# Pooled attention with a routed feed-forward layer: queries loaded as whole rows and half of them moved between partition groups, values loaded by one transfer

## The chip, the core and the metric

The kernel runs on one core of a Trainium2 chip. The metric is the device time of one execution in microseconds (us). The core has TensorE (PE in the profile; its weight loads are PEld), VectorE (DVE), ScalarE (ACT), GpSimd (POOL) and the queue of SyncE (SP), which issues nearly all transfers here. Each engine works through its own instructions in order; semaphores tie the engines together.

## What is computed

Eight batches of eight heads. The queries of neighbouring positions are averaged in twos (1152 rows become 576), attention is computed without a mask, and the result of all heads side by side (576 rows of 512) goes through a routed layer: a score for each row, and the 128 rows with the highest score get a gated two-layer feed-forward update.

```python
q_pool = q.reshape(B, H, S // 2, 2, D).mean(axis=3)        # B=8, H=8, S=1152, D=64
scores = q_pool @ k.T / sqrt(D)
x = softmax(scores) @ v                                    # -> (B, 576, 512)
s = x @ w_gate
top = argpartition(-s[b], 128)[:128]
out[b] = x[b];  out[b, top] += sigmoid(s[b, top]) * (relu(x[b, top] @ w1) @ w2)
```

## The kernel before

**Pairs and halves.** Two heads (j = 0, 1) of a batch make a pair; there are 32 pairs. The 128 partitions hold head j's 64 dimensions at rows 64j to 64j+63. A pair is worked in two halves, one for each 288 of its 576 pooled queries: half number h = 2n + s belongs to pair n, and s = 0 or 1 picks the columns of the transposed queries `qT`. I call halves with s = 0 even and those with s = 1 odd.

**One half, in the order of `run` (L1562).** The order on every engine is that in which this loop writes the instructions; nothing reorders them. In each half:
- `scores` (L853): PE multiplies the transposed keys `kT` with `qT` (columns of this half) in nine chunks of 128 keys, ACT exponentiates each chunk out of PSUM into `p` (L876). PSUM holds four such chunks.
- `side_by_side` (L938, even halves) or `spread` (L953, odd halves): four small ACT copies between groups of 32 partitions.
- `units("mid")`: pieces of the routing of an earlier batch, among them PE's feed-forward products.
- `gated` (L1035, DVE), then `folded` (L901): POOL adds two thirds of `p` (L908), DVE transposes and sums (L913, twice) and joins the sums (L923). These give the softmax denominators.
- `units("sums")`: more routing, then `multiplied` (L976, POOL).
- `added` (L944, DVE) and `prepare_pair` (L761) for the next pair, in even halves only.
- `weighted` (L878) of the half before: PE multiplies `p` with the values, ACT copies the result out of PSUM (L895), POOL adds its two parts (L897); `drained` (L966): DVE transposes it.
- `normalized` or `divided`, and `units("end")`: rank comparisons (L1145 to L1164) and searches (L1229) of the routing, on DVE.

So PE alternates between the scores of half h and the weighted sum of half h - 1, and `qT` and `kT` of pair n + 1 are made in pair n's even half, a whole half before PE first reads them.

**Loads.** `load_pair` (L735) is called in the odd half, for the pair after the next: four transfers for keys and four for queries, one for each group of 32 partitions (head j, dimensions 0 to 31 or 32 to 63). Each moves, for each of 32 partitions, 36 pieces of 32 numbers (128 bytes). `load_values` (L748) follows, four transfers of 32 partitions whose rows are whole (2304 bytes for each head), for the next pair. All are issued by SP. The first pair is loaded and prepared by other code (L776 to L851).

**Preparation.** `prepare_pair` adds neighbouring queries on POOL (L767: 128x576), transposes the keys in blocks of 32x32 on DVE (L770: 128x1152) into columns ordered (c, g, i), and the queries likewise (L774: 128x576). A block transposition stays within its group of 32 partitions, and since the load has put each group's own 32 dimensions there, the result lies where `scores` reads it. `kb`, `kT` and `qT` have two buffers each; `qb` and `qp` have one.

**Routing.** For each batch b the routing starts at half 8b + 10 and goes on in pieces for some twenty halves. Batches 0 to 5 are updated in twos, with seven block products on PE (L1437) in each layer, at halves 28 and 31, 44 and 47, 60 and the end. The transposition of the picked rows (L1284) stands in `units("sums")` of an odd half.

Of the kernel before, what the change touches and what calls it, by code (L numbers as in the profile page):

```python
# [10 lines left out]
P = 128  # L11
BLK = 32

G = 3
F32 = mybir.dt.float32
# [12 lines left out]
def _any_scores(  # L28
# [451 lines left out]
    in_pair = [(j, t) for j in range(2) for t in range(NF)] + [(0, NF)]  # L480
    upcoming = load_pair(*pairs[0])
    run(prepare_pair(upcoming))
    preparing = iter(())
    routing = iter(())
# [23 lines left out]
    for n, (b, hp) in enumerate(pairs):  # L508
        pair = upcoming
        run(preparing)  # L510
        if hp == 0:
            x = xpool.tile([P, NT, Dm], F32, name="x")
        for i, (j, t) in enumerate(in_pair):
            now = {"pair": pair, "j": j, "t": t, "x": x}
            advance(now)
            if two is not None and two["t"] == NF and two["pair"]["hp"] == NPAIR - 1:
                run(routing)
                routing = routed(two["pair"]["b"], two["x"])
            one, two = now, one
            if i == 0 and n + 1 < len(pairs):  # L520
                upcoming = load_pair(*pairs[n + 1])
                preparing = prepare_pair(upcoming)
            if n == 0 and i == 0:
                load_weights()
            if i >= 3:
                next(preparing, None)
            next(routing, None)
# [7 lines left out]
class _Plain:  # L535
# [199 lines left out]
    def load_pair(self, b, hp):  # L735

        nc = self.nc
        kb = self.load.tile([P, self.KB, BLK], F32, name="kb")
        qb = self.load.tile([P, self.QB, 2, BLK], F32, name="qb", bufs=1)
        for j, ds, rows in self.quarters():  # L740
            of = self.k[b, 2 * hp + j, :, ds]
            nc.sync.dma_start(kb[rows, :, :], of.rearrange("(i n) d -> i n d", i=BLK))
        for j, ds, rows in self.quarters():
            of = self.q[b, 2 * hp + j, :, ds].rearrange("(i m) d -> i m d", i=BLK)
            nc.sync.dma_start(qb[rows, :, :, :].rearrange("i n r d -> i (n r) d"), of)
        return {"k": kb, "q": qb, "b": b, "hp": hp}

    def load_values(self, pair):  # L748


        nc, hp = self.nc, pair["hp"]
        v_sb = pair["v"] = self.load.tile([P, 2, self.NC, self.D], F32, name="v_sb", bufs=2)
        of = self.v[pair["b"], 2 * hp : 2 * hp + 2]
        of = of.rearrange("j (i g c) d -> g i j c d", i=BLK, c=self.NC)
        for g in range(P // BLK):
            nc.sync.dma_start(
                v_sb[g * BLK : (g + 1) * BLK, :, :, :].rearrange("i j c d -> i j (c d)"),
                of[g].rearrange("i j c d -> i j (c d)"),
            )

    def prepare_pair(self, pair):  # L761

        nc = self.nc
        qp = self.load.tile([P, self.QB, BLK], F32, name="qp", bufs=1)
        kT = pair["kT"] = self.load.tile([P, self.S], F32, name="kT")
        qT = pair["qT"] = self.load.tile([P, self.Sp], F32, name="qT")
        nc.gpsimd.tensor_tensor(  # L767
            out=qp[:, :, :], in0=pair["q"][:, :, 0, :], in1=pair["q"][:, :, 1, :], op=ALU.add
        )
        nc.vector.transpose(  # L770
            kT.rearrange("p (c g i) -> p c g i", c=self.NC, i=BLK),
            pair["k"].rearrange("p (g c) d -> p c g d", c=self.NC),
        )
        nc.vector.transpose(qT[:, :], qp.rearrange("p n d -> p (n d)"))  # L774

    def load_first(self, b, hp):  # L776

# [784 lines left out]
    def run(self):  # L1562
        nc = self.nc
        pairs = [(b, hp) for b in range(self.B) for hp in range(self.NPAIR)]
        n_halves = 2 * len(pairs)
        halves = []
        self.routing, self.waiting = [], set()
        upcoming = self.load_first(*pairs[0])
        self.first_constants()
        self.prepare_first(upcoming)  # L1570
        self.constants()
        loaded = self.load_pair(*pairs[1]) if len(pairs) > 1 else None
        self.load_gate()
        weights = self.weight_loads()
        sums = self.weight_sums() if self.paired else iter(())
        for h in range(n_halves):
            n, s = divmod(h, 2)
            if s == 0:
                pair = upcoming
                if pair["hp"] == 0:  # L1580
                    part = self.ffn.tile([P, self.NPAIR, self.QB], F32, name="part")
                pair["part"] = part
            else:
                loaded = None
                if n + 2 < len(pairs):
                    loaded = self.load_pair(*pairs[n + 2])
                if n + 1 < len(pairs):
                    self.load_values(upcoming)
                if n > 1:
                    self.stored(halves[h - 4]["pair"])  # L1590
            if h > 1:
                next(weights, None)

            if 5 < h < 14 or 18 < h < 23:
                for _ in range(2 - s):
                    next(sums, None)
            half = {"pair": pair, "s": s}
            halves.append(half)
            self.scores(half)
            if h > 1:  # L1600

                of = halves[h - 2 - s]["pair"]
                if s == 0:
                    of["groups"] = self.side_by_side(of["sum"].rearrange("p j n -> p (j n)"))
                else:
                    self.spread(of)
            self.units("mid")
            if h > 2:
                self.gated(halves[h - 3])
            self.folded(half)  # L1610
            if h > 2:
                self.scored(halves[h - 3])
            self.units("sums")
            if h > 1:
                self.multiplied(halves[h - 2])
            if h > 1 and s == 0:
                last = halves[h - 1]["pair"]
                last["total"] = self.added(last["groups"])
            if s == 0 and loaded:
                upcoming = loaded  # L1620
                self.prepare_pair(upcoming)
            if h > 0:
                self.weighted(halves[h - 1])
                self.drained(halves[h - 1])
            if h > 2 and s == 1:
                self.normalized(halves[h - 2]["pair"])
            if h > 3 and s == 0:

                self.divided(halves[h - 3]["pair"])
            self.units("end")  # L1630
        for _ in weights:
            pass
        for _ in sums:
            pass

        def pieces(unit, n=None):
            for i, _ in enumerate(unit):
                if i + 1 == n:
                    break


        left = [unit for _, unit, _ in self.routing]
        old = left.pop() if left else iter(())
        older = left.pop() if left else iter(())
        assert not left
        self.gated(halves[-3])
        pieces(old, 1)
        self.weighted(halves[-1])
        self.drained(halves[-1])
        self.multiplied(halves[-2])  # L1650
        self.multiplied(halves[-1])
        self.scored(halves[-3])
        self.gated(halves[-2])
        pieces(older, 1)
        self.normalized(halves[-1]["pair"])
        self.gated(halves[-1])
        self.scored(halves[-1])
        _, new, _ = self.routing.pop()

        pieces(new, 1)  # L1660
        pieces(old, 1)
        for half in (halves[-3], halves[-1]):
            self.divided(half["pair"])
            self.stored(half["pair"])
        pieces(older, 2)
        pieces(new, 1)
        pieces(old, 1)
        pieces(older, 1)
        pieces(new, 3)
        pieces(older, 4)  # L1670
        pieces(old, self.NFC // 2)
        pieces(new, 1)
        low = self.counted()
        pieces(old, self.NFC // 2 + 1)
        pieces(older)
        pieces(new, 2)
        pieces(old)
        count = self.outside(low)
        pieces(new, 10)
        found = nc.values_load(count[0:1, 0:1])  # L1680
        E = mybir.EngineType
        self.tc.mark_branch_hint_location("again", found, [E.PE, E.DVE, E.Pool, E.Activation, E.SP])
        pieces(new)
        return found
# [61 lines left out]
```

## Time and profile before

| what | value |
|---|---|
| median of 3 runs | 689.82 us (689.19 to 692.28) |
| the profiled execution | 689.66 us |
| its span in the profile | 687.9 us |
| granted TensorE clock, mean | 0.998 |
| busy PE, PEld | 678.0 us (99%), 564.4 us (82%) |
| busy DVE, ACT, POOL | 536.4 us (78%), 457.7 us (67%), 512.9 us (75%) |
| DMA | 101.22 MB in 397,059 packets, 377,232 of them under 512 bytes |
| share of the 16 DMA engines' time, SP's queue | 67.1% |
| start of one half's scores to the next half's, undisturbed | 8.73 us |

The profile is one execution. A row of its groups gives line, engine and operation, what it writes and reads, partitions x elements, the count, the busy time, the mean duration in ns, and the idle time of the engine just before it with the instruction that ended that idle time. A row of its timeline gives start, duration, engine, line and operation, with idle time and releaser in brackets. An engine's next instruction often starts some 0.07 us before the listed end of the last one, so in a chain the distance of starts is what counts.

### The profile page before, as it was taken

The page shows a single profiled execution, that of the slowest core. Times are in us where ns is not written, and L with a number is a line of the kernel's source. Part 1 is how long each engine was busy: PE and PEld are TensorE (multiplying, and loading weights), DVE is VectorE, ACT ScalarE, POOL GpSimd, SP SyncE. Part 2 cuts the span into 40 slices and gives each one's busy share as a digit, 9 for nine tenths or more (in the row PEclk, how much of TensorE's full clock was granted, in tenths as well). Part 3 has the DMA queues.
Part 4 walks back from the last instruction along what each step waited for, and adds up shares of the span by engine and source line. Part 5 has one row for each costly group of instructions (what it writes and reads, how often), then busy time and mean ns, then how long its engine had stood idle before and what let it go on. Part 6 is the DMA issues. An engine that isn't in the chain of part 4 may idle for free.

```text
span 687.9 us, 23660 instructions
## 1 busy us (share of the span) xinstructions
PE 678.0 (99%) x9972; PEld 564.4 (82%) x9972; DVE 536.4 (78%) x842; ACT 457.7 (67%) x998; POOL 512.9 (75%) x503
## 2 busy tenths in 40 slices
PE   9999999999999999999999999999999999999996
PEld 6668899989997998786888899777788899867776
DVE  3867888998999796786698977695879989688930
ACT  5677777777777783847777677583877777575220
POOL 4788888798887775867996978483999888569241
PEclk9999999999999999999999999999999999999999
DMA  9888878688779767953878787783777777644311
GB/s 173 158 176 182 209 143 202 130 155 165 138 167 171 159 136 140 229 101 80 227 129 176 135 166 148 139 197 64 158 190 171 140 152 163 118 116 118 81 47 36
DMA packets 397059, 101.22 MB, mean 147 GB/s; under 512 B 377232, under 2 KB 381200, under 8 KB 395664
## 3 DMA queue, kind: packets, MB, share of 16 engines
q1 hardware_dynamic: 395408, 95.13, 67.1%
q0 software_dynamic: 1296, 4.20, 1.9%
q8 instruction: 80, 1.31, 0.8%
q10 hardware_dynamic: 240, 0.30, 0.2%
q14 instruction: 35, 0.29, 0.1%
HBM read 81.97 MB, written 17.62 MB: 145 GB/s over the span
## 4 chain that ended last, share of the span: by engine, by line
PE 83%; DVE 4%; DMA 4%; issue 4%; POOL 3%; ACT 1%; SPq 0%; POOLq 0%; DVEq 0%; ACTq 0%
PE ps L887 36%; PE ps L869 36%; PE ps L1437 8%; DVE fold L913 2%; DMA out_dram<-xe,index 1%; PE ps L1312 1%; POOL acc L908 1%; ACT p L876 1%; DMA v_sb<-in_v_dram 1%; DMA lines<-row_rank 1%; PE ps L616 1%; DMA row_rank<-both 0%; POOL prod L976 0%; POOL s L1403 0%; DVE pick L1164 0%
## 5 line engine op out<-in xcount | busy, mean ns | idle before, releaser
L876 ACT ACTIVATE p<-ps 128x576 f32<-128x576 f32 x576 | 320.4, 699 | 2.4 <-PE ps L869 2.4
L887 PE MATMUL ps<-p,v_sb 64*64 64x288 f32 x4608 | 296.7, 403 | 2.0 <-DMA v_sb<-in_v_dram 2.0
L869 PE MATMUL ps<-qT,kT 64*64 64x288 f32 x4608 | 296.4, 403 | 0.7 <-DVE token L637 0.5
L908 POOL TENSOR_TENSOR acc<-p 128x576 f32<-128x576 f32 x192 | 272.0, 1444 | 26.7 <-ACT p L876 26.1
L887 PEld LDWEIGHTS ps<-p,v_sb 64*64 64x64 f32 x4608 | 233.7, 133 | 49.9 <-ACT p L876 13.3
L869 PEld LDWEIGHTS ps<-qT,kT 64*64 64x64 f32 x4608 | 229.3, 133 | 51.4 <-ACT p L876 4.6
L913 DVE TRANSPOSE_TENSOR_REDUCE fold<-p 128x54 f32<-128x1728 f32 x64 | 126.0, 1968 | 32.8 <-ACT p L876 32.8
L913 DVE TRANSPOSE_TENSOR_REDUCE fold<-acc 128x54 f32<-128x1728 f32 x64 | 124.7, 1948 | 27.3 <-POOL acc L908 27.3
L895 ACT COPY two<-ps 128x576 f32<-128x576 f32 x64 | 40.8, 637 | 139.0 <-PE ps L887 131.6
L897 POOL TENSOR_TENSOR av<-two 128x288 f32<-128x288 f32 x64 | 51.2, 800 | 68.7 <-ACT two L895 65.4
L767 POOL TENSOR_TENSOR qp<-qb 128x576 f32<-128x576 f32 x31 | 43.7, 1409 | 14.0 <-DMA qb<-in_q_dram 12.9
L976 POOL TENSOR_TENSOR prod<-avb,w_gate 128x288 f32<-128x288 f32 x64 | 51.7, 808 | 1.5 <-DVE red L1035 1.3
L966 DVE STREAM_TRANSPOSE avb<-av 128x288 f32<-128x288 f32 x64 | 29.0, 453 | 23.2 <-POOL av L897 22.8
L770 DVE STREAM_TRANSPOSE kT<-kb 128x1152 f32<-128x1152 f32 x31 | 42.1, 1357 | 0.0
L953 ACT ACTIVATE sums<-total,tiny 32x18 f32<-32x18 f32 x124 | 38.2, 308 | 2.3 <-DVE total L944 0.3
L1013 POOL TENSOR_TENSOR x<-avb,rec 128x576 f32<-128x576 f32 x30 | 34.8, 1160 | 0.0
L1164 DVE SCALAR_TENSOR_TENSOR pick<-sc_row,gate_sc,before 128x128 f32<-128x128 f32 (+1 forms) x40 | 31.3, 782 | 1.4
L938 ACT COPY groups<-sum 32x36 f32<-32x36 f32 x124 | 27.3, 220 | 2.4 <-DVE sum L923 0.7
L1035 DVE TENSOR_REDUCE red<-prod 128x9 f32<-128x288 f32 x64 | 27.7, 433 | 0.1
L1445 ACT COPY s<-ps 128x256 f32<-128x256 f32 (+1 forms) x27 | 11.4, 447 | 20.8 <-PE ps L1437 20.8
L774 DVE STREAM_TRANSPOSE qT<-qp 128x576 f32<-128x576 f32 x31 | 22.6, 730 | 2.1 <-POOL qp L767 2.0
L923 DVE TENSOR_REDUCE sum<-fold 128x18 f32<-128x108 f32 x64 | 21.9, 342 | 2.2
(136 smaller groups left out, 481.7 us busy)
## 6 DMA issues: line engine op xcount, KB each, us to landing
kb<-in_k_dram SPq DMA_DIRECT2D x124, 144.0 KB, 4.5
qb<-in_q_dram SPq DMA_DIRECT2D x124, 144.0 KB, 3.7
v_sb<-in_v_dram SPq DMA_DIRECT2D x124, 144.0 KB, 3.5
tw<-tw SPq DMA_DIRECT2D x10, 1024.0 KB, 7.0
out_dram<-x SPq DMA_DIRECT2D x128, 72.0 KB, 3.0
lines<-row_rank SPq DMA_DIRECT2D x7, 640.0 KB, 4.6
w<-in_moe_w_dram SPq DMA_DIRECT2D x8, 512.0 KB, 6.3
tw<-tw SPq DMA_DIRECT2D x8, 512.0 KB, 5.6
```

Of the source, the lines that this page charges most:

```text
L767: nc.gpsimd.tensor_tensor(out=qp[:, :, :], in0=pair["q"][:, :, 0, :], in1=pair["q"][:, :, 1, :], op=ALU.add)
L770: nc.vector.transpose(kT.rearrange("p (c g i) -> p c g i", c=self.NC, i=BLK), pair["k"].rearrange("p (g c) d -> p c g d", c=self.NC),)
L869: nc.tensor.matmul(sc[keys, j, 0:n], lhsT=pair["kT"][rows, c * P + keys.start : c * P + keys.stop], rhs=pair["qT"][rows, qs], start=True, ...
L876: nc.scalar.activation(p[:, c // G, c % G, :, :], sc[:, :, 0:n], AF.Exp, scale=self.scale)
L887: nc.tensor.matmul(av[j * self.D : (j + 1) * self.D, e, 0:n], lhsT=half["pair"]["v"][keys, j, c, :], rhs=half["p"][keys, c // G, c % G, j, :],
L895: nc.scalar.copy(two[:, :, :], av[:, :, 0:n])
L897: nc.gpsimd.tensor_tensor(out=half["av"][:, :], in0=two[:, 0, :], in1=two[:, 1, :], op=ALU.add)
L908: nc.gpsimd.tensor_tensor(out=acc[:, u, :], in0=units[:, 0, u, :], in1=units[:, 1, u, :], op=ALU.add)
L913: nc.vector.tensor_reduce(fold[:, a, :], of.rearrange("p u (m d) -> p (u m) d", d=BLK), AX.X, ALU.add, apply_transpose=True,)
L953: self.nc.scalar.activation(tot[rows, :], pair["total"][:, j * self.QB : (j + 1) * self.QB], AF.Identity, bias=self.tiny[0:BLK, 0:1],)
L976: self.nc.gpsimd.tensor_tensor(out=pair["prod"][:, ns, :], in0=pair["avb"][:, ns, :], in1=self.w_gate[:, hp : hp + 1, :].broadcast_to([P, ...
L1437: nc.tensor.matmul(args[0], lhsT=args[1], rhs=args[2], start=k == 0, stop=k == n - 1)
```

## The change

- **Queries.** Each group of 32 partitions now loads whole rows: group g = 2j + s gets head j's queries of half s, 18 successive rows of 64 numbers (4608 bytes) for each partition. The sum on POOL has the same size. DVE's block transposition is now two of 128x288, one for each 32 of the 64 dimensions. In the group of half 0 the low 32 dimensions land in their place, in the group of half 1 the high ones; the other two quarters of each head are in the wrong group of partitions.
- **Moves.** Two new steps in the odd half put that right. `copied_across`, after `spread`: ACT copies 32x288 from the high rows to the low rows for each head. `turned_across`, after `units("sums")`: DVE transposes 32x288 of `qp` once more for each head, from the low rows to the high rows. Both write the `qT` that PE reads in the next half.
- **Values and keys.** The values are loaded by one transfer of 128 partitions with rows in natural order, so the keys' transposition writes its columns in the order (c, i, g): successive elements lie four apart instead of side by side.

```diff
@@ load_pair
-        qb = self.load.tile([P, self.QB, 2, BLK], F32, name="qb", bufs=1)
+        qb = self.load.tile([P, self.HB, 2, self.D], F32, name="qb", bufs=1)
...
-        for j, ds, rows in self.quarters():
-            of = self.q[b, 2 * hp + j, :, ds].rearrange("(i m) d -> i m d", i=BLK)
-            nc.sync.dma_start(qb[rows, :, :, :].rearrange("i n r d -> i (n r) d"), of)
+        of = self.q[b, 2 * hp : 2 * hp + 2].rearrange("j (i s m) d -> j s i (m d)", i=BLK, s=2)
+        for g in range(P // BLK):
+            rows = slice(g * BLK, (g + 1) * BLK)
+            nc.sync.dma_start(qb[rows, :, :, :].rearrange("i n r d -> i (n r d)"), of[g // 2, g % 2])
@@ load_values
-        of = of.rearrange("j (i g c) d -> g i j c d", i=BLK, c=self.NC)
-        for g in range(P // BLK):
-            nc.sync.dma_start(
-                v_sb[g * BLK : (g + 1) * BLK, :, :, :].rearrange("i j c d -> i j (c d)"),
-                of[g].rearrange("i j c d -> i j (c d)"),
-            )
+        nc.sync.dma_start(
+            v_sb.rearrange("p j c d -> p j (c d)"), of.rearrange("j (p c) d -> p j (c d)", c=self.NC)
+        )
@@ prepare_pair
-        qp = self.load.tile([P, self.QB, BLK], F32, name="qp", bufs=1)
+        qp = pair["turn"] = self.load.tile([P, self.HB, self.D], F32, name="qp", bufs=1)
...
         nc.vector.transpose(
-            kT.rearrange("p (c g i) -> p c g i", c=self.NC, i=BLK),
+            kT.rearrange("p (c i g) -> p c g i", c=self.NC, i=BLK),
             pair["k"].rearrange("p (g c) d -> p c g d", c=self.NC),
         )
-        nc.vector.transpose(qT[:, :], qp.rearrange("p n d -> p (n d)"))
+        for e in range(2):
+            nc.vector.transpose(qT[:, self.half_of(e)], qp[:, :, e * BLK : (e + 1) * BLK])
+
+    def half_of(self, s):
+        return slice(s * self.HALF, (s + 1) * self.HALF)
+
+    def crossing(self, j):
+
+        return slice(j * self.D, j * self.D + BLK), slice(j * self.D + BLK, (j + 1) * self.D)
+
+    def copied_across(self, pair):
+
+        qT = pair["qT"]
+        for j in range(2):
+            low, high = self.crossing(j)
+            self.nc.scalar.copy(qT[low, self.half_of(1)], qT[high, self.half_of(0)])
+
+    def turned_across(self, pair):
+
+        qp = pair.pop("turn")
+        for j in range(2):
+            low, high = self.crossing(j)
+            self.nc.vector.transpose(pair["qT"][high, self.half_of(0)], qp[low, :, BLK:])
@@ run, in the loop over halves
                 else:
                     self.spread(of)
+            if s == 1 and "turn" in upcoming:
+                self.copied_across(upcoming)
             self.units("mid")
...
             self.units("sums")
+            if s == 1 and "turn" in upcoming:
+                self.turned_across(upcoming)
             if h > 1:
                 self.multiplied(halves[h - 2])
```

## The prediction

> **What bounds the kernel now.** I read the page first: busy shares, then the chain that ended last.
>
> ```profile
> span 687.9 us, 23660 instructions
> ...
> PE 678.0 (99%) x9972; PEld 564.4 (82%) x9972; DVE 536.4 (78%) x842; ACT 457.7 (67%) x998; POOL 512.9 (75%) x503
> ...
> PE 83%; DVE 4%; DMA 4%; issue 4%; POOL 3%; ACT 1%; SPq 0%; POOLq 0%; DVEq 0%; ACTq 0%
> ```
>
> PE is never free for long, so a change to loads can win little, and whatever makes PE wait is added in full. The list of waits gives what there is to win: PE waits for `v_sb` 2.0 us, and POOL waits 12.9 us for `qb`, off PE's path. The timeline of PE shows two disturbed starts of scores for which a late `v_sb` is named: half 24 comes 10.89 us after half 23 and half 40 comes 9.96 us after half 39, where 8.73 is usual. Together that is 3.4 us.
>
> Next the timeline of one undisturbed odd half, h = 3, with the start of half 4 (column one is the start):
>
> ```profile
> 30.96 4.54 PE L869 MATMUL ps<-qT,kT 64*64 64x288 f32 x72
> ...
> 31.77 4.99 ACT L876 ACTIVATE p<-ps 128x576 f32<-128x576 f32 x9
> ...
> 36.79 1.27 ACT L953 ACTIVATE sums<-total,tiny 32x18 f32<-32x18 f32 x4
> 36.80 1.98 DVE L913 TRANSPOSE_TENSOR_REDUCE fold<-p 128x54 f32<-128x1728 f32 x1 [1.60 <-ACT p L876]
> ...
> 38.70 1.94 DVE L913 TRANSPOSE_TENSOR_REDUCE fold<-acc 128x54 f32<-128x1728 f32 x1
> ...
> 39.69 4.56 PE L869 MATMUL ps<-qT,kT 64*64 64x288 f32 x72
> 39.99 0.64 ACT L895 COPY two<-ps 128x576 f32<-128x576 f32 x1 [1.93 <-PE ps L887]
> ...
> 40.67 0.36 DVE L923 TENSOR_REDUCE sum<-fold 128x18 f32<-128x108 f32 x1
> ```
>
> Count from T = 30.96, the start of half 3's scores. The exponentials end at T+5.8, so the first fold on DVE starts there; the join of the sums (L923) starts at T+9.71. PE starts the next half's scores at T+8.73. **DVE finishes an odd half's folds after PE has already gone on to the next pair.** Today nobody on PE waits for that. `turned_across` stands in DVE's queue right behind L923, and its result is read by PE's first scores of the next half.
>
> **The change part by part.** The rows for the sizes:
>
> ```profile
> L966 DVE STREAM_TRANSPOSE avb<-av 128x288 f32<-128x288 f32 x64 | 29.0, 453 | 23.2 <-POOL av L897 22.8 <-POOL gate_sc L1093 0.4
> ...
> L770 DVE STREAM_TRANSPOSE kT<-kb 128x1152 f32<-128x1152 f32 x31 | 42.1, 1357 | 0.0
> ...
> L1284 DVE STREAM_TRANSPOSE xeT<-pick 128x512 f32<-128x512 f32 x6 | 7.2, 1194 | 0.0
> ...
> L1126 DVE COPY sc_row<-ps 128x288 f32<-128x288 f32 x1 | 0.7, 694 | 0.1
> ...
> L938 ACT COPY groups<-sum 32x36 f32<-32x36 f32 x124 | 27.3, 220 | 2.4 <-DVE sum L923 0.7
> ```
>
> *Loads.* The queries' 31 x 4 transfers lose their 1,152 pieces of 128 bytes each (142,848 of the 377,232 packets under 512 bytes) for 32 rows of 4608 bytes each; the values' four transfers become one. SP issues as many query transfers and three fewer value transfers a pair. A new transfer's landing is bounded by the rows for `v_sb` (144 KB, 3.5 us) and for `tw` (1024 KB, 7.0 us); the values, 576 KB, are loaded more than one half of 8.73 us before use, so either end is hidden. I credit at most the 3.4 us above. If that cover went, the price would be such a wait again.
>
> *POOL's sum* keeps its 576 elements: 1.41 us, bounds 1.16 (L1013) to 1.44 (L908). POOL is off PE's path in an even half. Nothing.
>
> *The copies on ACT.* No row has 32x288. Bounds 0.22 us (L938, 32x36) and 0.64 us (L895, 128x576); by length between them about 0.4, so 0.8 a pair. They follow `spread`, which ends at T+7.1, and end at T+7.9. What they read was transposed half a pair before. Behind them in ACT's queue are the routing's `mid` pieces and L895, before which ACT idles 1.93 us (in the excerpt, the L895 that starts at 39.99): covered, at either bound. Without that cover the next exponentials would start 0.8 us late, and PE with them.
>
> *The queries' transposition* becomes two of 128x288: 0.36 (the distance of starts from L966 to the next instruction in a chain, 34.44 to 34.80) + 0.42 instead of 0.72 (L774, which the timeline shows at 33.78), so +0.06 us in the even half.
>
> *The keys' transposition* now writes four elements apart. Nearest rows: L1126, a copy that writes 18 apart, takes 694 ns for 288 elements; by L843 (552 ns for 384) and L828 (357 for 192) a contiguous copy of 288 takes 455, so 0.83 ns an element more, 0.96 us for 1152. L1284, which reads and writes four apart, takes 1194 where 512 by L774's rate take about 655: 1.05 ns an element, 1.2 us. Lower bound nothing, since the same elements are written and no gain is to be had. I take 1.0 us (nearer to both rows). [...]
>
> *`turned_across`.* Two transpositions of 32x288 on DVE. By L966 0.36 + 0.42 = 0.78; bounds half of that and, at L1126's price, 1.4. It waits for the copies (T+7.9) and stands behind L923, whose next instruction can start at T+9.71+0.26 = T+9.97 (as at 31.92 to 32.18). It ends at T+10.75, PE starts about 0.12 later (as L1117 after DVE's L1106, 643.15 to 643.28), at T+10.87 instead of T+8.73: **2.14 us of idle PE at each pair boundary.** Queued behind it on DVE are `drained`, `normalized`, the routing's `end` pieces and `gated`; POOL's L976 waits for `drained`. All of them fit before the next fold.
>
> *How often.* 31 boundaries (the first pair has none of its own). At two, halves 31 and 47, PE has 12.3 us of L1437 in the odd half and DVE is in time: no stall. 29 x 2.14 = 62.1.
>
> *Where DVE or POOL is later than in half 3.* In the trace the same end point lies 1.7 to 7.4 us after the next start of scores, 114.1 us over the 29 boundaries. Much of that is a backlog of routing work carried through several halves; once PE waits for DVE at every boundary, it is shed there. What remains is work within one pair. From an even start T, the last DVE instruction before the odd half's folds ends at T+12.97 (half 2: 35.20 - 22.23), and those folds are due at T+8.73+5.84 = T+14.57. The dearer keys and queries take 1.06 of these 1.6; after a stall L895 has long run, so the exponentials start some 0.45 us earlier, and 0.99 us are free. Beyond that:
> - rank comparisons at the end of an even half, 3.54 us (140.62 to 144.16), before boundaries 15, 23, 39 and 55: 4 x 2.55 = 10.2;
> - the search L1229, 1.12 us, at 17, 25, 41, 57: 4 x 0.13 = 0.5; a weight difference L720, 1.1 us, in six odd halves: 0.7;
> - L1284 in six odd halves, straight ahead of the new step: 6 x 1.04 = 6.2;
> - POOL late with L908 in halves 33 and 49 (next lines): 2 x 2.46 = 4.9;
> - the first boundary, 4.54 in all, and the last, 4.20: 4.5 more than counted.
>
> ```profile
> 320.86 4.54 PE L869 MATMUL ps<-qT,kT 64*64 64x288 f32 x72
> ...
> 331.04 1.98 DVE L913 TRANSPOSE_TENSOR_REDUCE fold<-acc 128x54 f32<-128x1728 f32 x1 [2.33 <-POOL acc L908]
> ...
> 333.05 0.34 DVE L923 TENSOR_REDUCE sum<-fold 128x18 f32<-128x108 f32 x1
> ```
>
> Here the join starts 12.19 after half 33's scores instead of 9.71.
>
> *Sum.* 62.1 + 10.2 + 1.2 + 6.2 + 4.9 + 4.5 - 3.4 = 85.7. The profiled execution took 689.66 us (span 687.9), 0.16 from the median of 689.82. 689.66 + 85.7 = **775 us**.
>
> The granted clock stays at 1.00 in the trace also around half 24, where PE twice idles under 1 us; I count no change. [...]
>
> **Rivals.**
> - *The backlog is not shed:* the stalls are the lateness of the trace as it is, 114.1 + 6.2 - 3.4 = 117: 807 us. For it: DVE's share of 78% leaves little, and it gains 1.9 us a pair. Against: DVE idles 1.6 us before the fold of half 3, so it catches up.
> - *Only ACT's cover fails:* DVE's step is in time for some reason, but the copies delay the exponentials: 31 x 0.8 = 25, 689.7 + 25 - 3.4 = 711 us. Against: the 1.93 us of idle ACT.
> - *The step is in time and loads win (the other side):* `turned_across` would have to be done on DVE by T+8.6, that is start by T+7.9, 2.1 us earlier than its place behind L923 allows. If it were, PE would keep its 8.73 and lose the late values: 689.66 - 3.4 = 686 us. For it: DVE does idle before the folds. Against: the written order.
>
> **Numbers.** Forecast 0.81, backlog not shed 0.10, ACT alone 0.04, in time 0.05. A measurement of this kernel tells about 0.5% from no change; 686 is at that edge, so its 0.05 is 0.03 faster and 0.02 the same, and 0.95 is slower. Bounds within the forecast: cheap turns -11 and free keys -5 give 759, dear turns (29 x 0.6) +17 and keys at 1.2 us +2 give 794. The range takes these, something for the shedding on both sides, and the first rival: 752 to 807.
>
> **What would show it.** Right: scores (L869) wait for DVE's `qT` at 29 boundaries, about 2.1 us at the plain ones, some 85 in all; PE's share falls to about 88%; L770 takes 2.3 us, the new transpositions 0.36 to 0.45, the copies 0.4; POOL's wait for `qb` is gone and so are about 140,000 packets. Wrong: PE's distance of halves stays 8.73 at even halves, or the wait named is ACT's, or the shortfall lies within the halves.

## The result, and the profile after

The changed kernel takes **813.02 us** (median of 6 runs, 810.72 to 814.53). The kernel before took 690.22 us beside it (6 runs, 689.05 to 692.83). The ratio is 1.1738, with a 95% interval of 1.1695 to 1.1782: slower by 17%, where 775 was forecast with a range up to 807. The profiled execution took 813.33 us, with a mean granted clock of 0.959 against 0.998 before.

In the new file the lines have moved: scores L869 are L889, products with the values L887 are L907, exponentials L876 are L896, the evictions L895 are L915, folds L913 are L933, the join of the sums L923 is L943. `copied_across` is L787 and `turned_across` L794. The page of the changed kernel, busy shares, clock, the chain and the groups:

```profile
span 811.6 us, 23665 instructions
PE 720.8 (89%) x9972; PEld 537.6 (66%) x9972; DVE 583.8 (72%) x935; ACT 495.5 (61%) x1060; POOL 517.0 (64%) x503
PEclk9999999989999899999889999999999989999999
PE 40%; DVE 25%; ACT 15%; POOL 10%; issue 5%; DMA 3%; SPq 1%; POOLq 0%; ACTq 0%; DVEq 0%
L889 PE MATMUL ps<-qT,kT 64*64 64x288 f32 x4608 | 337.7, 432 | 82.5 <-DVE qT L794 81.9
L768 DVE STREAM_TRANSPOSE kT<-kb 128x1152 f32<-128x1152 f32 x31 | 78.6, 2534 | 0.0
```

PE's share falls from 99% to 89% and the share of the chain that ran on PE from 83% to 40%. Every other engine's share falls too: no engine is busy throughout any more, and the chain passes from one to the next. PE sat 81.9 us before scores until DVE had done L794. The list of waits says how often:

```profile
PE ps L889 <- DVE qT L794: 81.9, 29, 5.0
```

29 waits: one at each of the 29 boundaries that the prediction counted, and none at the two (behind halves 31 and 47) that it left out. Now the same odd half 3 as before, from the timeline:

```profile
39.31 4.54 PE L889 MATMUL ps<-qT,kT 64*64 64x288 f32 x71
...
45.15 1.98 DVE L933 TRANSPOSE_TENSOR_REDUCE fold<-p 128x54 f32<-128x1728 f32 x1 [0.78 <-ACT p L896]
46.44 0.88 ACT L787 COPY qT<-qT 32x288 f32<-32x288 f32 x2
47.05 1.94 DVE L933 TRANSPOSE_TENSOR_REDUCE fold<-acc 128x54 f32<-128x1728 f32 x1
...
49.02 0.33 DVE L943 TENSOR_REDUCE sum<-fold 128x18 f32<-128x108 f32 x1
49.38 0.97 DVE L794 STREAM_TRANSPOSE qT<-qp 32x288 f32<-32x288 f32 x2
...
49.91 5.09 PE L889 MATMUL ps<-qT,kT 64*64 64x288 f32 x72 [1.69 <-DVE qT L794]
...
59.09 4.64 PE L889 MATMUL ps<-qT,kT 64*64 64x288 f32 x72
...
69.81 5.09 PE L889 MATMUL ps<-qT,kT 64*64 64x288 f32 x72 [1.72 <-DVE qT L794]
```

Count from T = 39.31, the row with 71 of the half's 72 matmuls (the first ran at 39.07). The join starts at T+9.71, where it did before; in half 5, whose 72 matmuls stand in one row from 59.09 on, it starts at T+9.84. The copies on ACT have been over since T+8.0. The two turns run from T+10.07 to T+11.04. PE starts head 0's scores as soon as head 0's turn is done (T+10.60) and stands once more inside that half, for head 1's: 5.09 us for 72 matmuls instead of 4.54. From 49.91 to 69.81, one pair of halves, are 19.90 us; before, two halves of 8.73 were 17.46. **A plain boundary costs 2.44 us.**

The second thing is in the clock. PE's windows around one boundary, columns window, length, busy PE (matmuls), granted clock, DMA share, GB/s:

```profile
436.00:440.00 4.00, 3.28 (x56) 1.00 0.84 181
440.00:441.00 1.00, 0.00 (x0) 1.00 0.67 105
441.00:443.00 2.00, 2.00 (x16) 0.64 0.90 141
443.00:445.00 2.00, 2.00 (x24) 0.50 0.42 67
445.00:447.00 2.00, 2.00 (x40) 1.00 0.00 0
```

PE idles for 1.72 us, and 0.6 us after it starts again the clock falls to 0.50: 24 matmuls in 2 us instead of 40. The trace has 13 such falls between 28 and 738 us, each of 3.4 or 6.8 us. The kernel before had none until 685 us. The rows of scores hit by one last 6.1 to 7.6 us instead of 5.09; the excess adds up to 21.0 us (20.6 in an expectation below).

The whole difference of spans, 811.6 - 687.9 = 123.7 us, taken apart by the trace of after:

| term | predicted, us | measured, us |
|---|---|---|
| 29 plain boundaries | 62.1 (2.14 each) | 70.8 (2.44 each) |
| boundaries where DVE or POOL is later still | 27.0 | 33.1 |
| granted clock | 0 | 21.0 |
| late `v_sb` no longer late | -3.4 | -3.4, from the trace of before |
| sum | 85.7 | 121.5 |
| outside these terms | | 2.2 |

The list of waits of after has no row for `v_sb`, so the 3.4 us are counted as gone. Of the last 2.2 us, 2.0 lie at the ends of the run: the first scores start 0.80 us later than before (7.97 instead of 7.17), half 0 takes 1.61 us longer, with the clock at 0.50 from 8.1 to 11.5 us, and the stretch behind the start of the last scores is 0.4 us shorter.

### The profile page after: what moved, and what is told of

The parts are those of the page before. It is cut to its first block, busy times and chain, and to the rows that moved or that the text cites. A ratio compares the mean times of both kernels' runs of the same rounds, so it can differ in the third digit from the quotient of the medians.

```text
span 811.6 us, 23665 instructions
## 1 busy us (share of the span) xinstructions
PE 720.8 (89%) x9972; PEld 537.6 (66%) x9972; DVE 583.8 (72%) x935; ACT 495.5 (61%) x1060; POOL 517.0 (64%) x503
## 4 chain that ended last, share of the span: by engine, by line
PE 40%; DVE 25%; ACT 15%; POOL 10%; issue 5%; DMA 3%; SPq 1%; POOLq 0%; ACTq 0%; DVEq 0%
PE ps L889 18%; DVE fold L933 14%; PE ps L907 13%; ACT p L896 13%; PE ps L1457 8%; POOL acc L928 8%; DVE kT L768 3%; DVE qT L794 2%; DVE sum L943 1%; ACT two L915 1%; DVE pick L1184 1%; PE ps L1332 1%; DVE xeT L1304 1%; DVE qT L773 1%; DMA out_dram<-xe,index 1%
## 5 line engine op out<-in xcount | busy, mean ns | idle before, releaser
L889 PE MATMUL ps<-qT,kT 64*64 64x288 f32 x4608 | 337.7, 432 | 82.5 <-DVE qT L794 81.9
L896 ACT ACTIVATE p<-ps 128x576 f32<-128x576 f32 x576 | 325.1, 685 | 115.0 <-PE ps L889 114.4
L889 PEld LDWEIGHTS ps<-qT,kT 64*64 64x64 f32 x4608 | 219.0, 142 | 190.7 <-DVE qT L794 104.6
L907 PE MATMUL ps<-p,v_sb 64*64 64x288 f32 x4608 | 299.4, 403 | 0.0
L907 PEld LDWEIGHTS ps<-p,v_sb 64*64 64x64 f32 x4608 | 219.5, 133 | 60.1 <-ACT p L896 9.6
L933 DVE TRANSPOSE_TENSOR_REDUCE fold<-p 128x54 f32<-128x1728 f32 x64 | 126.4, 1975 | 139.1 <-ACT p L896 138.9
L933 DVE TRANSPOSE_TENSOR_REDUCE fold<-acc 128x54 f32<-128x1728 f32 x64 | 124.4, 1943 | 8.8 <-POOL acc L928 8.8
L915 ACT COPY two<-ps 128x576 f32<-128x576 f32 x64 | 40.8, 638 | 112.1 <-PE ps L907 111.5
L768 DVE STREAM_TRANSPOSE kT<-kb 128x1152 f32<-128x1152 f32 x31 | 78.6, 2534 | 0.0
L986 DVE STREAM_TRANSPOSE avb<-av 128x288 f32<-128x288 f32 x64 | 29.1, 455 | 17.4 <-POOL av L917 16.6
L794 DVE STREAM_TRANSPOSE qT<-qp 32x288 f32<-32x288 f32 x62 | 29.1, 470 | 1.9
L787 ACT COPY qT<-qT 32x288 f32<-32x288 f32 x62 | 26.6, 429 | 3.8 <-DVE qT L773 2.3
L773 DVE STREAM_TRANSPOSE qT<-qp 128x288 f32<-128x288 f32 x62 | 25.2, 439 | 0.0
L1184 DVE SCALAR_TENSOR_TENSOR pick<-sc_row,gate_sc,before 128x128 f32<-128x128 f32 (+1 forms) x40 | 23.5, 588 | 1.4
```

What stands on the lines that cost most here:

```text
L768: nc.vector.transpose(kT.rearrange("p (c i g) -> p c g i", c=self.NC, i=BLK), pair["k"].rearrange("p (g c) d -> p c g d", c=self.NC),)
L794: self.nc.vector.transpose(pair["qT"][high, self.half_of(0)], qp[low, :, BLK:])
L889: nc.tensor.matmul(sc[keys, j, 0:n], lhsT=pair["kT"][rows, c * P + keys.start : c * P + keys.stop], rhs=pair["qT"][rows, qs], start=True, ...
L896: nc.scalar.activation(p[:, c // G, c % G, :, :], sc[:, :, 0:n], AF.Exp, scale=self.scale)
L907: nc.tensor.matmul(av[j * self.D : (j + 1) * self.D, e, 0:n], lhsT=half["pair"]["v"][keys, j, c, :], rhs=half["p"][keys, c // G, c % G, j, :],
L915: nc.scalar.copy(two[:, :, :], av[:, :, 0:n])
```

## The experiments

The theory to test: nothing but `turned_across` in its place behind the folds makes the loss, by PE's waits and by the falls of the clock that these bring. The rivals: the keys' dearer transposition costs DVE the time; the copies on ACT do; the loads matter. All ratios are to the kernel before on the same chip; the chips differ by up to 0.9% (medians of before 685.84 to 691.97), so ratios are compared, not times.

### Parts alone

**e1_keys_values_only**: before, with the values' single transfer and the keys in the order (c, i, g).

```diff
-            kT.rearrange("p (c g i) -> p c g i", c=self.NC, i=BLK),
+            kT.rearrange("p (c i g) -> p c g i", c=self.NC, i=BLK),
...
+            v_sb.rearrange("p j c d -> p j (c d)"), of.rearrange("j (p c) d -> p j (c d)", c=self.NC)
```

> The kernel before with the values' single transfer and the keys' columns written four apart; queries as before. Theory (PE waits for the transposition across, and falls to half clock after the waits): DVE pays 31 x 1.18 = 37 us more but nobody on PE waits for it, so 687 to 693. Rival (the dearer key transposition is what makes DVE late): 690 + 37 = 727, or at least above 700.

687.71 us, ratio 1.0002 (0.9983 to 1.0021). The group of the keys in its profile:

```profile
L767 DVE STREAM_TRANSPOSE kT<-kb 128x1152 f32<-128x1152 f32 x31 | 73.2, 2361 | 0.0
```

2361 ns against 1357 before: the step of four on the writing side costs 1.00 us for 1152 elements, as taken in the prediction. DVE pays 31 us more, and PE, 99% busy, doesn't notice.

**e2_queries_only**: after, with these two edits taken back.

> The changed kernel with values and keys as before; only the queries' part is left. Theory: the waits stay, only the places where an even half has no room left win back up to 1.18 us each, some 8 to 16 boundaries: 795 to 808, granted clock still 0.95 to 0.97. Rival (key transposition): 813 - 37 = 776 or less.

804.62 us, ratio 1.1686 (1.1649 to 1.1723), clock 0.957. Nearly the whole loss is the queries'. In its list of waits:

```profile
PE ps L892 <- DVE qT L797: 72.7, 29, 4.1
```

With the keys at 1356 ns PE waits 9.2 us less than in after; by the ratios the two differ by 0.0052, 3.6 us, which the intervals do not quite tell apart. So by the waits the keys' price, nothing in e1, begins to count once PE waits for DVE; the times alone don't show it.

**e3_copies_without_turn**: after, with `turned_across` left out (the high rows of the first half's queries are not filled).

```diff
             if s == 1 and "turn" in upcoming:
-                self.turned_across(upcoming)
+                upcoming.pop("turn")
```

> The changed kernel without the transposition across (the high rows of the first half's queries stay wrong); the copies on ACT, the loads and the keys stay. Theory: all of the loss goes, 686 to 693, granted clock 0.998. Rival (the copies push the exponentials): 690 + 31 x 0.86 = 717 or, with the last forecast's figure, 711.

692.86 us, ratio 1.0074 (1.0050 to 1.0099), clock 0.999. Without the two turns 0.17 of the 0.174 is gone, falls of the clock included. The 0.7% left has ACT in it:

```profile
PEld ps L889 <- ACT two L915: 5.1, 5, 1.4
```

In five halves, where the routing gives ACT its own work, the copies push the eviction L915 late.

**e9_turn_without_copies**: the opposite, `copied_across` left out (the low rows of the second half's queries are not filled).

> The changed kernel without the copies on ACT (the low rows of the second half's queries stay wrong); the transposition across stays behind the join of the sums. Theory: the wait is DVE's, ACT is covered, so 808 to 813 with the clock at 0.95 to 0.965. Rival (the copies have a part in the wait): 790 or less.

816.39 us (814.01 to 819.82), ratio 1.1885 (1.1844 to 1.1926): no faster than after, so the rival that the copies make the wait falls. It came out 3 us above the upper end that I expected, and by ratios above after itself. Its clock is 0.949, after's 0.959; 0.010 of 818 us is about 8 us, most of the 10 by which the ratios differ. PE's waits are the same in total (81.7 us against 81.9), but at the lower clock the matmuls of the scores are busy for 345.9 us instead of 337.7 (441 ns each on average against 432); with what a fall of the clock goes is shown further down, at the step that failed.

**e10_no_moves**: both moves left out (both missing quarters unfilled), loads, transpositions, keys and values as changed.

```diff
-                self.copied_across(upcoming)
...
-                self.turned_across(upcoming)
+                upcoming.pop("turn")
```

> The changed kernel without both moves (two quarters of the queries of each pair stay wrong): whole-row loads, two transpositions of 128x288, values and keys as changed. Theory: the loads win nothing that PE would see, 686 to 690, so that the run with the copies alone, 692.9, shows some 4 us that ACT's copies cost where ACT has no idle time. Rival (these 4 us come from the loads or the keys): 692 or more.

686.06 us beside 685.84, ratio 1.0001 (0.9987 to 1.0015). The page's chain line:

```profile
PE 90%; DMA 5%; issue 2%; POOL 2%; DVE 1%; ACT 1%; ACTq 0%; SPq 0%; POOLq 0%; DVEq 0%
```

So the new loads, with 140,368 packets fewer (397,059 to 256,691), win nothing that can be measured, and e3's 0.7% is the copies'.

### The clock

**e4_busy_in_the_wait**: after, with seven matmuls of ones that nobody reads (14 rows, 1.83 us in the trace) put into PE's queue where it waits, at every boundary that has a wait.

```diff
+                if s == 1 and h not in (31, 47) and h + 1 < n_halves:
+                    self.kept_busy()
...
+    def kept_busy(self):
+        ps = self.banks()[:, 0, 0:P]
+        for _ in range(7):
+            self.nc.tensor.matmul(ps, lhsT=self.ones[:, :], rhs=self.ones[:, :], start=True, stop=True)
```

> The changed kernel with seven extra matmuls of 128x128 by 128 columns of ones (about 1.6 us at full clock) behind the weighted sum of each odd half, except halves 31 and 47 and the last; they fall into the time in which PE waits. Theory: the clock falls because PE idles, so it stays near 0.99 and most of the 20 us of slow scores are won: 790 to 800; the end of the wait itself doesn't move. Rival (the slow scores have another cause, or gaps of up to 3.4 us left over by the filling are enough): 813, clock 0.96.

796.54 us (792.45 to 801.84), ratio 1.1553 (1.1511 to 1.1595). The median is as expected, the clock isn't: 0.977 in the profiled execution, the slowest (801.84 us), and 0.982 to 0.988 in the other three. The profiled one has eight falls left between 26 and 727 us, where the wait is longer than seven matmuls fill.

**e8_busy_all_the_wait**: the same with 8 to 19 matmuls where the wait of after is longer.

```diff
+        more = {1: 8, 7: 2, 9: 2, 11: 3, 13: 2, 15: 8, 19: 8, 21: 1, 23: 12, 25: 1, 27: 4, 33: 8, 35: 4}
+        more.update({39: 12, 43: 4, 49: 8, 51: 4, 55: 12, 57: 2, 59: 4, 61: 8})
+        for _ in range(7 + more.get(h, 0)):
```

> As the run with seven extra matmuls, with more of them (8 to 19) where the wait is longer, so that PE idles under 0.5 us at nearly every boundary. Theory (slow scores come from the clock, and the clock falls because of PE's idle time): granted clock 0.995 or more, the 20.6 us of slow scores are gone and nothing else changes: 789 to 794. Rival: the clock stays at 0.96 to 0.98 and the time at 796 to 813.

792.74 us (792.26 to 794.28), ratio 1.1458 (1.1394 to 1.1522), clock 0.998. Its clock by slices, and the boundary that fell to 0.50 in after (L780 are the added matmuls, L896 the scores, L914 the products):

```profile
PEclk9999999999999999999999999999999999999999
```

```profile
421.67 4.64 PE L914 MATMUL ps<-p,v_sb 64*64 64x288 f32 x72
426.24 1.83 PE L780 MATMUL ps<-ones 128*128 128x128 f32 x14
428.04 5.09 PE L896 MATMUL ps<-qT,kT 64*64 64x288 f32 x72
```

PE starts the scores no earlier than DVE lets it, but at full clock: 5.09 us where after took 6.54. Useless work makes the kernel 0.028 faster, 19 us, and no fall is left in the middle of the run. That the clock took some 20 of the 38 us missed is shown by taking its falls away.

### Another place for the moves

**e5_turn_between_folds**: `turned_across` called behind the first fold of the odd half, not behind both.

```diff
+                self.folded(half, upcoming if s == 1 and "turn" in upcoming else None)
...
+            if upcoming and a == 0:
+                self.turned_across(upcoming)
```

> The changed kernel with the transposition across moved ahead by one fold on DVE: behind the fold of p instead of behind the join of the sums, 2.3 us earlier. Theory (its place in DVE's queue decides): it then waits for the copies on ACT, which end 8.0 us after the odd half's scores start, so PE's start moves by some 0.4 us a boundary instead of 2.4; what remains are the boundaries with rank comparisons and the first, and few falls of the clock: 720 to 735. Rival (the place doesn't matter, the dearer instructions do): 805 to 813.

733.08 us, ratio 1.0595 (1.0536 to 1.0654), clock 0.985.

```profile
PE ps L889 <- DVE qT L794: 22.9, 14, 2.8
```

The step stands some 2.3 us earlier in the same queue (a fold of 1.94 us and the join), and of 29 waits 14 are left, of 82 us 23, of a loss of 17% 6%. The work is the same: when DVE reaches the step sets most of the loss.

**e6_all_in_even_half**: both moves made by DVE in the even half, right behind the other transpositions; no copies on ACT.

```diff
+        for j in range(2):
+            low, high = self.crossing(j)
+            nc.vector.transpose(qT[high, self.half_of(0)], qp[low, :, BLK:])
+            nc.vector.transpose(qT[low, self.half_of(1)], qp[high, :, :BLK])
```

> The changed kernel with both moves done on DVE in the even half, right behind the queries' transposition (two more transpositions of 32x288 in place of ACT's copies, and the two across there): nothing of the new pair is left for the odd half. Theory: PE waits for nothing; DVE pays 4 x 0.49 + 0.08 + 1.18 = 3.2 us a pair off PE's path, 636 of 690 us busy: 686 to 700. Rival (DVE has no room for it, the total of its work decides): above 715.

715.61 us, ratio 1.0346 (1.0288 to 1.0404): my expectation failed, the rival's figure was met. The page's busy shares and chain:

```profile
PE 690.3 (97%) x9972; PEld 519.1 (73%) x9972; DVE 623.0 (87%) x997; ACT 461.0 (65%) x998; POOL 511.3 (72%) x503
DVE 51%; PE 31%; DMA 6%; POOL 6%; issue 4%; ACT 2%; SPq 0%; DVEq 0%; POOLq 0%; ACTq 0%
```

The long wait at the boundaries is gone, but with DVE at 87% its queue has become half of the chain.

**e7_even_half_old_keys**: e6 with the keys and values of before.

> As the run with everything in the even half, but with keys and values as before: DVE pays 2.0 us a pair, 600 of 690 us busy. Theory: 685 to 692, that is no worse than the kernel before, and better than the run with the dearer keys if that one is above it. Rival: above 705.

696.62 us, ratio 1.0074 (1.0045 to 1.0103): better than e6 by 0.027, or 19 us, but still slower than before and above what I expected. The dearer keys, free in e1 together with the values' transfer, cost 19 us here, where DVE has half of the chain. No version tried beats the kernel before, and e10 shows why none could by much: with the moves at no cost, the new loads give back nothing.

## Why the prediction was wrong, point by point

**The mechanism was right.** PE waits for `turned_across` at 29 boundaries, and e3 and e9 show that it is this step and no other. The rivals "only ACT's cover fails" (711) and "in time, and loads win" (686) fell; e10 shows that the loads would have won nothing even without the moves (ratio 1.0001).

**The step that failed** is "The granted clock stays at 1.00 in the trace also around half 24, where PE twice idles under 1 us; I count no change." It was a term set to zero from waits under 1 us, where the step added waits of 1.7 us and more. Measured: 21 us by the rows of scores in the trace of after, 19 us by e8. In after the clock fell after the wait of 1.72 us before half 38, but not after the waits of 2.57 to 2.66 us before halves 8 to 14, so no length of a single wait decides.

The trace of after shows what goes with a fall. All 29 changes of the clock in it lie whole multiples of 3.413 us apart: the falls at 393.78, 417.68, 441.57 and 465.46 are 23.89 to 23.90 apart, seven times that. Cut the trace at these points (columns as above):

```profile
127.54:130.96 3.42, 2.00 (x35) 1.00 0.95 247
130.96:134.37 3.41, 2.17 (x30) 1.00 0.03 10
438.16:441.57 3.41, 1.69 (x26) 1.00 0.72 113
```

The wait of 2.66 us before half 12 is split over two such windows, 1.42 and 1.24 us idle, and no fall follows; the 1.72 us before half 38 lie in one, and at its end the clock falls. Between 25 and 740 us of after, the clock fell at the end of every window at full clock with 2.05 us of idle PE or more and of none with less than 1.72; of nine windows between these two, two brought a fall. So in this trace where in the windows a wait lies counts as much as its length, and the same kernel can have more falls or fewer in another execution (clock 0.955 to 0.963 over the six of after). Without the slow clock the kernel takes e8's 793 us, inside the range.

**A plain boundary was 0.30 us too cheap**, 8.7 us in all. The prediction had "By L966 0.36 + 0.42 = 0.78" and a start 0.26 behind L923. The trace has the start 0.36 behind L943, and the turns 0.97 long: 0.10 + 0.19 us. In the trace of after each of the 62 turns writes from another group of 32 partitions on than the instruction before it, and each starts 0.03 us after the end of that one instead of 0.07 before. The timeline of e6 shows the same beside an instruction that does overlap:

```profile
68.70 0.34 DVE L947 TENSOR_REDUCE sum<-fold 128x18 f32<-128x108 f32 x1
68.97 0.39 DVE L968 TENSOR_REDUCE total<-groups 32x36 f32<-32x144 f32 x1
...
72.33 0.47 DVE L776 STREAM_TRANSPOSE qT<-qp 32x288 f32<-32x288 f32 x1
72.83 0.47 DVE L777 STREAM_TRANSPOSE qT<-qp 32x288 f32<-32x288 f32 x1
73.31 0.47 DVE L776 STREAM_TRANSPOSE qT<-qp 32x288 f32<-32x288 f32 x1
```

L968 has 32 partitions too, but begins at the first one, like L947: it starts 0.07 us before L947's listed end. Each turn begins elsewhere than the last and starts 0.01 to 0.03 us after its end. Shape alone is not the reason: in after the same L986 (128x288) starts 0.07 us before the listed end of L773, which begins in its group (43.61 against 43.68), and 0.03 us after the end of the second turn, which doesn't (50.38 against 50.35).

**Boundaries that are later still**: 33.1 us instead of 27.0. The six transpositions `xeT` (1.03 us each, predicted 1.04) and POOL's two late sums (2.2 each, predicted 2.46) were right. The rank comparisons gave about 12 instead of 10.2, the weight differences 4.1 instead of 0.7, the search 1.7 instead of 0.5, the first and last boundary 4.2 instead of 4.5. I read the misses that cost as one assumption, the 0.99 us of room that I gave DVE before the folds. In the trace DVE idles 0.78 us before the first fold of half 3, where the keys took 2.35, and 0.20 before that of half 5, where they took 2.78. The 0.45 us credited for earlier exponentials did not come: those of half 4 start 0.85 us after PE's weight loads go on with head 1 (50.41 to 51.26), as those of half 5 in the trace of before start 0.83 after its scores (48.42 to 49.25). The keys took 2.53 us on average in after instead of the 2.36 used for this, and e2 shows PE waiting 9.2 us less where they take 1.36. What lengthens them from 2.36 in e1 to 2.53 is open.

**"The backlog is not shed" (807)** is close to the time, for another reason. Its stalls would add up to 114.1 + 6.2 = 120.3 us, the forecast's to 89.1; measured without the clock are 70.8 + 33.1 = 103.9. Of the 14.8 over the forecast, 8.7 are the dearer turns. The longest single wait is 5.0 us where the rival needs 7.4. So most of the backlog is shed, not all.

**Small terms.** The copies take 0.43 us each (0.4 said); they were not quite free, 0.7% by e3 and e10. POOL's wait for `qb` is gone. The 3.4 us credited for late values can't be seen in e1 or e10: the new loads alone win nothing there.

## What to carry to other kernels

A step put at the end of an engine's in-order queue in one period, whose result another engine reads first thing in the next, costs its lateness in every period (here 2.44 us at a plain boundary); ask when the engine reaches the step, not how busy it is (DVE stood at 78% and had no room at that point, and at 87% its queue made half of the chain). In after, waits of 1.7 us and more that come back on the matmul engine about every 20 us go with a clock of 0.959, some 20 us on top of 104; for such waits the clock is a term with bounds, not nothing. Fewer and larger DMA pieces were worth nothing here (e10, ratio 1.0001), where PE waited 2.0 us in all for a transfer of values.

## What the runs showed of the hardware that was not expected

- In after the matmul clock changed only at steps of 3.413 us. It fell to 0.50, for one or two steps, at the end of every step at full clock with 2.05 us of idle PE or more, of two of nine with 1.72 to 2.00 and of none with less (25 to 740 us). With the waits partly filled by matmuls of ones it fell 8 times instead of 13 (e4, clock 0.977 against 0.959), with all of them filled not before 788 us of 791 (e8, 0.998).
- A 32x288 transposition on DVE across groups of 32 partitions takes 0.47 us (L794 in after), a 128x288 one within them 0.44 (L773); the price of the move is the lost overlap with its neighbours, some 0.1 us each (starts 0.48 to 0.50 us apart in e6, where 0.07 of overlap would make it 0.40).
- Writing four elements apart costs a transposition on DVE 1.0 us for 1152 elements, 0.87 ns an element (2361 against 1357 ns, e1 and before).
